# GpSimd takes q's product with its decay, the state's decay and small copies in a gated linear attention kernel

## The chip, the cores and the metric

The kernel runs on one core of one Trainium2 chip. The metric is the device time of one execution in microseconds (us); the median of three runs of the kernel before is 304.74 us (304.49 to 304.91). A core has five engines that work from queues of their own and wait for each other by semaphores: TensorE (in the profile PE, its weight loads PEld), VectorE (DVE), ScalarE (ACT), GpSimd (POOL) and SyncE (SP), which here issues the DMAs.

## The reference

Four sequences of 768 tokens with 8 heads of 48 features go through a gated linear attention and then through a block with a convolution and a gate:

```
f = 1 / (1 + exp(-f_logit))
for t in range(768):                                  # per sequence and head
    state = f[t][:, None] * state + outer(k[t], v[t]) # 48 x 48
    y[t] = q[t] @ state
x = y with the heads side by side                     # 768 x 384
h = max(x @ w_in, 0)                                  # 768 x 1024
conv = sum over 3 taps of conv_w[tap] * h shifted along the tokens
out = (h * sigmoid(conv)) @ w_out                     # 768 x 384
```

## The kernel before, in words

The attention is worked in 24 chunks (n = 0 to 23; four sequences of six chunks with 128 tokens each, c = 0 to 5 within a sequence). Per chunk, ScalarE turns the logits into ln(1 + exp(-f)) (L530, L534), and these are summed along the tokens, either by TensorE with a triangular matrix (L556, the first nine chunks) or by a scan on VectorE (L563). ScalarE takes two exponentials of the sum: with a plus sign for k (L565) and with a minus sign for q (L567), into the two halves of one buffer `e`, of which there are two. k and q lie side by side in one buffer `kq`, 128 partitions x 1024 numbers, and VectorE multiplies it by `e` in one instruction (L572). The last column of q's exponential is the decay over the whole chunk; a copy keeps it in `ft_all` (L569).

TensorE turns k (L587) and multiplies k by q for the scores (L594). VectorE copies the scores under a mask (L602), a copy brings the turned k from PSUM (L598), TensorE forms the products of k and v (L622) and of the scores and v (L614). VectorE adds the state's two halves (L635, L638), and the state is multiplied by its decay (L642 on VectorE, or L644, four activations on ScalarE), which the next chunk's L635 and TensorE's carry (L658) read. The result leaves PSUM as a rounded part (L671) and a rest (L673).

Two halves of a sequence make eight units u. In each, eight blocks f of 128 hidden features are computed as nine matmuls with split weights (L711), clipped by ScalarE into `hb` (L721), convolved by one ScalarE and two VectorE instructions (L727, L731), and gated in pairs (L735, L737). `hb` has two columns ahead of the tokens: for the first half of a sequence they are set to zero (L698), for the second half they are copied from the end of the first (L701), and the clipping waits for that. The output takes 24 tiles with 24 matmuls each (L767), from a rounded part (L754) and a rest (L758) of the gated features, and a copy (L773) ahead of the DMA. The weights come as 64-bit floats and are split during the first 60 us (L411 to L458).

`ORDER` is a list, written out, of all 1231 operations by number. Each engine's queue is that list with the other engines' work left out; a letter behind a number chooses the engine where an operation may run on several, and a number behind the dot chooses the buffer. An engine that waits for one operation holds up all that stands behind it.

Of the kernel before, what the change touches and what calls it, by code (L numbers as in the profile page):

```python
# [55 lines left out]
342.0 853 789.1 788.1 372.1 373 343.0 814 133.1 374 330 725.1 809 131 726 331v 790 375 132 835 346 332 347 810 348  # L56
405.1 392v 827 352.0 360.0 828 333 387.2 801.0 349 370.2 815 829 334 350 361.0 800.0 791.1 376.0 816 792 378.0 585 407
793.1 358.1 583 802 586 377.0 854 134 406.1 830 582 795.1 587 849 359.1 794.1 584 408.1 882 409 393 135 796 840 379.1
362 425 396.0 363 803.1 380 364 817 365 366 797.0 883.0 381 423.0 367.1 397.0 410 426.0 382 368 870.1 411 884 836 427
394.1 841 869 855 384 395v.0 871 414.0 856 441.3 385 398 872.1 415.1 875.0 383 386 885 873 459 888.1 876 908 842 399  # L60
# [3 lines left out]
905 593 916 419v 900 442.1 461 912 906 451.1 446 421.0 435 137 436 860 463 478.0 917 953.1 138 861v.1 496 948.0 422  # L64
907 448.0 949 894 438 449.0 922.0 954 466.0 475.0 479 452 493.1 494 467.0 961.1 458.0 960 918 950.0 913 439 550 966.0
962 462 497.1 440 498 974.1 951 967 973 437v 919 952 979.0 920 975 453 929.1 481 464.1 454 980 514 465.0 484.0 480 455
512.3 468 549.1 500 955 476.3 987.0 923 976 862 456 515.0 485.1 596 992.1 986 930.1 598 988 989 977 981 925.0 956 516
978 968 982 469 470 532 482.0 472 924 957 483.0 503.0 993 612.2 486 941.0 595 504.0 926 599 518 471 473.1 969 931.1
927.1 487 499v 474 613 928 488 597 533.1 990 994 513.0 958 501.1 489 490 502v.0 614 521.0 983 530.0 505 942.0 594
943.0 959 1011 491 534 492 535 984 522.1 932 506 963 995 517 507 944 985 536 519.0 945.1 509 520.0 996 551.0 539.0 615  # L70
531.2 1037 523 935.1 946 991 616.1 1012.0 508 933.0 524 510 964 934 1043.1 525 1013 511 965 602 970 527 1044 971 537.1
548.3 997 1017.1 600 538v.0 604 998 601 937.0 605 972 1018 617 620.2 936.0 603 540.0 1014.1 938 1019 552 1020 554
1030.1 939.0 1024 1050 940 1045 1015 528.2 1025.0 1031 529 526 1021 1032 1016 541 618 1033 557.0 1022 542 555.0 558.1
# [921 lines left out]
```

## Time and profile before

| | |
|---|---|
| median of three runs | 304.74 us |
| span of the profiled execution, first to last instruction | 301.5 us |
| median less that span | 3.24 us |
| TensorE busy | 293.8 us, 97% |
| VectorE busy | 255.3 us, 85% |
| ScalarE busy | 241.5 us, 80% |
| GpSimd busy | 2.8 us, 1% |
| granted clock of TensorE, mean | 0.996 |

The profile gives the execution's own time as its span; what lies around it is known only as the difference to the runs. A busy engine is one with an instruction running. TensorE's matmuls overlap and their ends are modelled, so a busy TensorE isn't proof that it works at its peak. Idle time of TensorE has the instruction behind the arrow as its releaser.

### The profile page before, as it was taken

How to read it: one execution, taken by the hardware profiler on the slowest of the kernel's cores; microseconds unless marked ns; L12 is line 12 of the kernel's file. 1: busy time of each engine (PE TensorE's matmuls, PEld its weight loads, DVE VectorE, ACT ScalarE, POOL GpSimd, SP SyncE). 2: the span in 40 equal slices, each digit the busy share in tenths (PEclk: the TensorE clock that was granted, in tenths of full speed). 3: DMA queues.
4: the chain of work that ended last, by engine and by line, in shares of the span. 5: the costliest groups of instructions: out<-in, count | busy, mean ns of one | idle time of the engine just before them, and what ended most of it. 6: DMA issues, size and time to landing. Idle time of an engine off the chain costs nothing. (4 is left out here: it accounts for less than half of the span.)

```text
span 301.5 us, 10047 instructions
## 1 busy us (share of the span) xinstructions
PE 293.8 (97%) x4319; PEld 276.6 (92%) x4319; DVE 255.3 (85%) x413; ACT 241.5 (80%) x482; POOL 2.8 (1%) x16
## 2 busy tenths in 40 slices
PE   8989999999999999999999999999999999999994
PEld 5867798999999999999999999989999999999993
DVE  3788999999999998999999996778985498498740
ACT  5787989999957999989979965876957797779460
POOL 3000000000000000000000000000000000000000
PEclk9999999999999999999999999999999999999998
DMA  6995799501650337522462454356041620212511
GB/s 216 393 358 185 267 299 383 156 2 32 165 217 0 99 133 231 180 80 72 133 202 49 160 164 122 99 156 195 8 145 21 185 70 28 96 54 97 192 54 58
DMA packets 19268, 43.38 MB, mean 144 GB/s; under 512 B 2684, under 2 KB 10004, under 8 KB 19220
## 3 DMA queue, kind: packets, MB, share of 16 engines
q1 hardware_dynamic: 19076, 42.50, 42.9%
q8 instruction: 35, 0.57, 0.8%
q10 hardware_dynamic: 144, 0.20, 0.2%
q14 instruction: 13, 0.11, 0.1%
HBM read 35.61 MB, written 4.72 MB: 134 GB/s over the span
## 5 line engine op out<-in xcount | busy, mean ns | idle before, releaser
L711 PE MATMUL mm<-xT,wi 128*128 128x384 f32 x576 | 107.3, 340 | 0.1
L711 PEld LDWEIGHTS mm<-xT,wi 128*128 128x128 f32 x576 | 100.5, 188 | 1.1 <-ACT hb L721 0.2
L731 DVE SCALAR_TENSOR_TENSOR g<-hb,cw,g 128x384 f32<-128x384 f32 (+1 forms) x128 | 73.8, 613 | 8.2 <-ACT g L727 7.9
L767 PE MATMUL mm<-wo,gh 128*128 128x384 f32 x384 | 70.9, 337 | 0.0
L767 PEld LDWEIGHTS mm<-wo,gh 128*128 128x128 f32 x384 | 66.5, 188 | 0.3
L721 ACT ACTIVATE hb<-mm 128x384 f32<-128x384 f32 x64 | 31.2, 488 | 16.6 <-PE mm L711 16.1
L727 ACT ACTIVATE g<-hb,cw 128x384 f32<-128x384 f32 (+1 forms) x64 | 37.4, 613 | 2.1 <-DVE gl L758 1.9
L767 PE MATMUL mm<-wo,gl 128*128 128x384 f32 x192 | 37.2, 338 | 0.0
L758 DVE TENSOR_TENSOR gl<-g,gh 128x1024 fp32r<-128x1024 f32 (+2 forms) x28 | 29.5, 1065 | 8.1 <-ACT gh L754 6.0
L767 PEld LDWEIGHTS mm<-wo,gl 128*128 128x128 f32 x192 | 33.4, 188 | 0.1
L572 DVE TENSOR_TENSOR kq<-kq,e 128x1024 f32<-128x1024 f32 x24 | 29.1, 1214 | 5.1 <-DMA kq<-in_kq_dram 5.1
L737 DVE SCALAR_TENSOR_TENSOR g<-g,hb 128x768 f32<-128x768 f32 (+1 forms) x32 | 30.1, 955 | 2.8 <-ACT g L735 2.5
L754 ACT CAST gh<-g 128x1024 fp32r<-128x1024 f32 (+2 forms) x28 | 25.8, 932 | 7.8 <-PE mm L767 4.6
L735 ACT ACTIVATE g<-g 128x768 f32<-128x768 f32 (+1 forms) x32 | 26.4, 840 | 0.0
L614 PE MATMUL Y<-am,v 64*64 64x64 f32 (+1 forms) x768 | 23.6, 219 | 0.0
L602 DVE COPY_PREDICATED am<-mask,S 128x512 f32<-128x512 uint8 x24 | 17.6, 733 | 1.9 <-PE S L594 1.8
L614 PEld LDWEIGHTS Y<-am,v 64*64 64x64 f32 (+1 forms) x768 | 18.8, 127 | 0.0
L673 DVE TENSOR_TENSOR xT<-Y,xT 112x512 fp32r<-112x512 f32 x24 | 16.3, 681 | 2.1 <-ACT xT L671 2.1
L563 DVE TENSOR_TENSOR_SCAN fb<-runs,fb 128x512 f32<-128x512 f32 x15 | 18.0, 1213 | 0.0
L594 PE MATMUL S<-kq 48*64 48x64 f32 x768 | 16.7, 221 | 1.0 <-DVE kq L572 0.9
L622 PEld LDWEIGHTS Y<-v,kp 64*48 64x48 f32 (+1 forms) x704 | 13.6, 127 | 3.5 <-issue 2.5
L594 PEld LDWEIGHTS S<-kq 48*64 48x64 f32 x768 | 13.9, 134 | 3.1 <-DVE kq L572 2.0
(100 smaller groups left out, 351.0 us busy)
## 6 DMA issues: line engine op xcount, KB each, us to landing
kq<-in_kq_dram SPq DMA_DIRECT2D x23, 512.0 KB, 6.0
v<-in_v_dram SPq DMA_DIRECT2D x24, 192.0 KB, 5.5
out_dram<-ob SPq DMA_DIRECT2D x23, 192.0 KB, 2.4
kq<-in_moe_w_in_dram SPq DMA_DIRECT2D x6, 512.0 KB, 5.1
kq<-in_moe_w_out_dram SPq DMA_DIRECT2D x6, 512.0 KB, 4.2
...
```

What stands on the lines that cost most here:

```text
L572: ox = plan.op("DVE", 1222, lambda e, X=X, E=E: nc.vector.tensor_tensor(buf(X), buf(X), buf(E), ALU.mult), ka, need=[o2] + ld_x, use=[X, E])
L594: o = nc.tensor.matmul(scores()[t, j, p, :], buf(X)[r, 0, p, t], buf(X)[r, 1, p, t], start=True, stop=True)
L614: o = nc.tensor.matmul(out_of(Y, p, j, w, z), buf(V).rearrange("p h d -> p (h d)")[t, h * D:h * D + w], buf(AM)[t, j, p, :], start=x == 1 ...
L711: nc.tensor.matmul(buf(ph)[:, :HS], wi[:, t, wl, f * P:(f + 1) * P], x_view(pl, u)[:, t, xl, :], start=(i == 0), stop=(i == 3 * KT - 1))
L721: nc.scalar.activation(hb[:, 2:HS + 2], buf(ph)[:, :HS], AF.Relu, scale=0.5)
L727: o = pl.op("ACT", 620, lambda e, cv=cv, hb=hb, n=n, f=f: nc.scalar.activation(cv(), hb[:, 1:n + 1], AF.Copy, scale=cw[:, 1, f:f + 1]), ke ...
L731: o = pl.op("DVE", 617, lambda e, cv=cv, hb=hb, n=n, f=f, w=w, sh=sh: nc.vector.scalar_tensor_tensor(cv(), hb[:, sh:n + sh], cw[:, w, f:f ...
L735: o = pl.op("ACT", 846, lambda e, cv=cv: nc.scalar.activation(cv(), cv(), AF.Tanh), key, need=last, use=[("g", u)], mode="T")
L737: gates[u, fp] = pl.op("DVE", 960, lambda e, cv=cv, fp=fp, n=n: nc.vector.scalar_tensor_tensor(cv(), cv(), 1.0, h_b[:, fp:fp + 2, 1:n + 1] ...
L754: o = pl.op("ACT", 180 + 110 * nn * NF // 128, lambda e, hv=hv, src=src: nc.scalar.copy(hv(), src()), key, need=[gates[v, fp] for fp in ra ...
L758: los.append(pl.op("DVE", 150 + 134 * nn * NF // 128, lambda e, hv=hv, lv=lv, src=src: nc.vector.tensor_tensor(lv(), src(), hv().bitcast(F ...
L767: nc.tensor.matmul(buf(po)[:, :DM], view(g)[:, f, :], wo[:, f, wl, :], start=(i == 0), stop=(i == 3 * NF - 1))
```

## The change

- L572 becomes two instructions, q's half and k's half. q's half runs on GpSimd in all 24 chunks, k's on VectorE. k's half needs k's exponential alone. The scores (L594) need both, the carry (L658) q's, the turn of k (L587) k's.
- The copy into `ft_all` (L569), the state's decay (L642, L644) and the two columns of `hb` (L698, L701) run on GpSimd, each in one instruction, in all chunks and units: 24 copies, 20 decays, 16 memsets and 16 copies.
- The rests of the gated features (L758) may run on GpSimd by the new code, but the new order leaves all of them on VectorE.
- The new `ORDER` has 1255 operations. The remaining work stands in the same order on TensorE, VectorE, ScalarE and SyncE as before, the exponentials of L565 and L567 among it.

```diff
+    copy_on = dict(ACT=nc.scalar.copy, DVE=nc.vector.tensor_copy, POOL=nc.gpsimd.tensor_copy)
+    tt_on = dict(DVE=nc.vector.tensor_tensor, POOL=nc.gpsimd.tensor_tensor)
+    memset_on = dict(DVE=nc.vector.memset, POOL=nc.gpsimd.memset)
...
-        keep = plan.op(dict(ACT=190, DVE=110), 0, lambda e, E=E, b=b, c=c: (nc.scalar.copy if e == "ACT" else nc.vector.tensor_copy)(
+        keep = plan.op(dict(ACT=190, DVE=110, POOL=200), 0, lambda e, E=E, b=b, c=c: copy_on[e](
             ft_all[:, b, c, :], buf(E)[:, 1, :, P - 1]), ka, need=[o2], use=[E])
-        ox = plan.op("DVE", 1222, lambda e, X=X, E=E: nc.vector.tensor_tensor(buf(X), buf(X), buf(E), ALU.mult), ka,
-                     need=[o2] + ld_x, use=[X, E])
+        oq, ox = [plan.op(dict(DVE=690, POOL=1300), 0, lambda e, X=X, E=E, z=z: tt_on[e](
+            buf(X)[:, z], buf(X)[:, z], buf(E)[:, z], ALU.mult), ka, need=[o2 if z else o1] + ld_x, use=[X, E], new=z == 1) for z in (1, 0)]
...
-        o = plan.op("PE", 490, score, (n, "sc"), need=[ox], use=[X], take=[("S", SC)], mode="q", n=64)
+        o = plan.op("PE", 490, score, (n, "sc"), need=[oq, ox], use=[X], take=[("S", SC)], mode="q", n=64)
...
-                if e == "DVE":
-                    return nc.vector.tensor_tensor(new, new, ft, ALU.mult)
+                if e != "ACT":
+                    return tt_on[e](new, new, ft, ALU.mult)
...
-            stated[n] = plan.op(dict(ACT=760, DVE=353), 0, decay, ks, need=[o, keep])
+            stated[n] = plan.op(dict(ACT=760, DVE=353, POOL=600), 0, decay, ks, need=[o, keep])
...
-                    oe = pl.op("DVE", 100, lambda e, fp=fp: nc.vector.memset(h_b[:, fp:fp + 2, 0:2], 0.0), key,
+                    oe = pl.op(dict(DVE=100, POOL=100), 0, lambda e, fp=fp: memset_on[e](h_b[:, fp:fp + 2, 0:2], 0.0), key,
...
-                    oe = pl.op(dict(ACT=200, DVE=110), 0, lambda e, fp=fp: (nc.scalar.copy if e == "ACT" else nc.vector.tensor_copy)(
+                    oe = pl.op(dict(ACT=200, DVE=110, POOL=200), 0, lambda e, fp=fp: copy_on[e](
                         h_b[:, fp:fp + 2, 0:2], h_b[:, fp:fp + 2, HS:HS + 2]), key, need=[gates.get((u - 1, fp))])
```

## Rows read from the trace of the kernel before

**Rows 1.** The page's head and its busy time (us, share, instructions).

```profile
span 301.5 us, 10047 instructions
...
PE 293.8 (97%) x4319; PEld 276.6 (92%) x4319; DVE 255.3 (85%) x413; ACT 241.5 (80%) x482; POOL 2.8 (1%) x16
```

**Rows 2.** Windows: stretch, us, busy us of PE, PEld, DVE, ACT, POOL; clock, DMA.

```profile
25.00:110.00 85.00, 84.68 (x1399) 77.20 (x1398) 84.52 (x133) 75.59 (x163) 0.00 (x0) 1.00 0.51 169
110.00:180.00 70.00, 69.91 (x1287) 67.21 (x1286) 67.46 (x106) 64.50 (x117) 0.00 (x0) 1.00 0.44 140
180.00:301.50 121.50, 116.90 (x1236) 114.38 (x1234) 87.03 (x140) 83.43 (x161) 0.00 (x0) 0.99 0.31 98
```

**Rows 3.** Groups by line and form, whole span: count, busy us, mean ns, idle before.

```profile
L572 DVE TENSOR_TENSOR kq<-kq,e 128x1024 f32<-128x1024 f32 x24 | 29.1, 1214 | 5.1 <-DMA kq<-in_kq_dram 5.1
...
L644 ACT ACTIVATE st<-st,ft_all 112x48 f32<-112x48 f32 x64 | 16.2, 329 | 0.7 <-DVE st L638 0.7
...
L569 ACT COPY ft_all<-e 128x4 f32<-128x4 f32 x22 | 4.1, 198 | 0.0
```

**Rows 4.** Groups by line on VectorE, 25 to 110 us.

```profile
L572 DVE TENSOR_TENSOR kq<-kq,e 128x1024 f32<-128x1024 f32 x10 | 12.1, 1216 | 0.0
...
L602 DVE COPY_PREDICATED am<-mask,S 128x512 f32<-128x512 uint8 x9 | 6.6, 733 | 0.0
L673 DVE TENSOR_TENSOR xT<-Y,xT 112x512 fp32r<-112x512 f32 x9 | 6.1, 682 | 0.3 <-ACT xT L671 0.3
...
L635 DVE TENSOR_TENSOR sh<-Y,st 112x192 f32<-112x192 f32 x7 | 2.4, 344 | 0.0
...
L638 DVE TENSOR_TENSOR st<-Y,sh 112x192 f32<-112x192 f32 x6 | 2.1, 346 | 0.0
...
L698 DVE MEMSET hb<- 128x4 f32 x7 | 0.4, 62 | 0.0
```

**Rows 5.** Groups by line on VectorE, 110 to 180 us.

```profile
L572 DVE TENSOR_TENSOR kq<-kq,e 128x1024 f32<-128x1024 f32 x8 | 9.7, 1212 | 0.7 <-DMA kq<-in_kq_dram 0.7
...
L642 DVE TENSOR_TENSOR st<-st,ft_all 112x192 f32<-112x192 f32 x3 | 1.1, 350 | 0.0
```

**Rows 6.** Groups by line and form on GpSimd, whole span.

```profile
L357 POOL MEMSET fg<- 128x512 f32 x2 | 1.0, 524 | 0.0
...
L785 POOL MEMSET mid<- 128x1 f32 x1 | 0.1, 98 | 0.0
```

**Rows 7.** Timeline, setup: start us, us, engine, line, operation, [idle before, releaser].

```profile
2.24 1.22 DVE L316 CAST idr<-ident 128x128 fp32r<-128x128 f32 x1
...
2.31 0.99 POOL L357 MEMSET fg<- 128x512 f32 x2
...
10.90 0.20 DVE L412 TENSOR_SCALAR gh<-gh 24x128 f32<-24x128 f32 x1
```

**Rows 8.** Timeline where TensorE waits, or nearly waits, for the products.

```profile
8.23 1.22 DVE L572 TENSOR_TENSOR kq<-kq,e 128x1024 f32<-128x1024 f32 x1 [4.40 <-DMA kq<-in_kq_dram]
...
12.21 0.59 ACT L567 ACTIVATE e<-mm 128x512 f32<-128x512 f32 x1
...
19.66 0.69 PE L594 MATMUL S<-kq 48*64 48x64 f32 x32 [0.53 <-DVE kq L572]
...
30.67 2.35 DVE L572 TENSOR_TENSOR kq<-kq,e 128x1024 f32<-128x1024 f32 x2
...
31.69 1.12 PE L452 MATMUL mm<-gh,ident 128*128 128x512 f32 x2 [0.26 <-ACT wi L457]
...
33.11 0.63 PE L587 MATMUL Y<-ident,kq 128*128 128x128 f32 x4
...
102.18 1.22 DVE L572 TENSOR_TENSOR kq<-kq,e 128x1024 f32<-128x1024 f32 x1
...
104.69 0.51 PE L594 MATMUL S<-kq 48*64 48x64 f32 x21
...
197.37 0.69 PE L594 MATMUL S<-kq 48*64 48x64 f32 x32 [0.33 <-DVE kq L572]
```

More of the change, by code (lines that the diff above doesn't have):

```diff
@@ L35 @@
 ORDER = """
[20 rows of a table removed]
[L56 to L60, printed above, removed]
[3 rows of a table removed]
@@ L64 @@
[L64 to L73, printed above, removed]
@@ L74 @@
-1026 1056.1 1027 1023 1028 1038.0 1089 543 1057 1029 556.0 544v 1058 1046 559 1063.0 619 545 624.1 560 1039 1034 561
[9 rows of a table removed]
-622 1204 1164 1145.1 1165 646 1146 1150 1213.0 1219.1 1214.1 1215.1 1151v.1 623 643 647 1152 1216 1205.0 1207 1221.0
-1217.0 1206.1 656.2 648.1 1218 1220.0 1208 1222 1225.1 1209.1 1223.1 1226.0 1224 655 649 1210 657 1227.0 658 650 659
-651 660 661.0 662 1211.1 1212 1228 1229v.0 1230
+91.0 92 93 139.0 158.1 45.0 94 100.1 96 140.0 7.1 159.1 97.1 23.1 95.0 10.0 24 141.0 4.0 142.0 8.1 177.2 143 5.0 98
@@ new lines @@
+160.1 145p 146v 99.0 102 6.0 144p 149.0 46.0 161.1 147.0 150.0 162 179.0 47 148.0 48 164p 165v 3.0 180.0 151 181 49
+50.0 168.0 103 51 687p 152 9.0 34.0 153 101 169.1 166.1 35 155 52 167.0 178.2 53.0 154p 109.0 25.0 0.0 196.0 104.0 54
+26 11.0 156.0 170 111 157 107 234.3 198.1 163p 182p 171 28 183p 184v 172 187.0 199.0 27.0 55.2 185.0 188.0 105 106.0
+29.0 1.0 186.0 217.0 173p 36.1 189 108.1 200 174 218.1 190 112 236.1 191 215.1 201p 219 37 197.1 175 56 193 113.0 110
+176 30.0 251.2 202p 203v 216.0 12.3 38.0 237.0 206.0 238 40.1 204.1 194 32.1 31 195 39 207.0 592 253.0 726p 240p 241v
@@ new lines @@
+116 13 33 593 192p 41.1 221p 222v 588 205.0 239p 591 220p 713p 58.0 254.0 223.0 57.0 255 225.0 59 117.1 589 208 42 65
+226.1 291.0 61 209 60 256p 114 2.0 292.1 43.1 62 224.0 210 590 115.0 63 293 64 212 257p 258v 244.0 235.2 213.1 123.1
+227 14.1 44 124 272.0 211p 214 125 118.0 245.0 73.0 242.1 273.0 228 15 714.1 120 274 243.0 83 67.0 17 16.0 82 719.0
+229 715 119 68 230p 246 18.0 720 70 231 247 261.0 66.1 232 270.1 248 71 289.0 126 233 21.0 262.1 249 700p 69 127 19.1
+250 72 594 22 259.0 252.0 20 84.0 727.0 271.2 85.0 308.3 121 87 598 688.1 597 86 728 595 122 276p 277v 693.0 599 689
@@ new lines @@
+596 310 275p 690.0 290.3 706.1 260.0 691 694 295p 296v 695 701.0 716 692 721 717 707 278.1 311.0 696 263 294p 718 702
+312 697 280.0 264 722 732.0 698 281.0 265 314p 315v 299.0 279.0 267 699 266p 282 268.0 300.1 757.1 751p 729 269 733
+723 703 283 724 297.0 730 752.0 284 298.0 704 734 725 708 301 758 705 285p 318.0 709 777p 286 731 753 88 302 778.0 735
+287 303 710 313p 754.1 736 711 305 288 737 783.1 712 402.3 779 738 306 780 307 796.0 759 755 764p 603 790p 784 760 601
+756 791.1 602 797 761 785 605 781 798 604 316.0 786 792 600 770.0 782 762 347.2 787 346.2 793 799 74 788 765.1 363.0
@@ new lines @@
+763 327.1 771 328.0 794 304p 309.1 800 830.0 772 795 766 829p 789 801 835.1 831 802 767 773 869.0 836 768 868p 76.1
+769 856.1 870 77 855p 774 79 874.0 75.1 857 80 775 78 861.1 875 776 81 843.0 862 319.0 803.1 89 848.1 805 842p 90 844
+329 807.0 804v.0 330.0 331 806v 745.0 333p 334v 808 317.0 365 739.1 320 348 809.0 332p 366.1 810 337.0 849 335.1
+740v.1 741.1 336.0 321 349.0 746v.0 367 350 338.1 832.0 128.0 322 742 837 129 352p 353v 850 876 403 324 845 368p 871
+356.0 384 382.3 339 325.0 130 811.1 747.0 369p 370v 323p 846 351p 404.0 847 863 326 858 748 340 405 872 743.0 357.0
@@ new lines @@
+823.0 744 354.0 877 813.1 812v.1 385.1 386 355.0 838 133.1 387p 341 749.1 833 131 750 342p 814 388p 389v 132 859 358
+343 359 834 360 420.1 406p 851 364.0 373.0 852 344 401.2 825.0 361 383.2 839 853 345 362 374.0 824v.0 815.1 390.0 840
+816 392.0 609 422 817.1 371.1 607 826 610 391.0 878 134 421.1 854 606 819.1 611 873 372.1 818v.1 608 423.1 906p 424
+407p 408v 135 820 864 393.1 375 441 411.0 376 827.1 394 377 841 378p 379 821.0 907.0 395 439.0 380.1 412.0 425p 442.0
+396 381 894.1 426p 427v 908 860 443 409.1 865 893p 879 398 410v.0 895 430.0 880 458.3 399 413 896.1 431.1 899.0 397p
@@ new lines @@
+400 909 897 477 912.1 900 932p 866 414 901 428.0 867 444p 933.0 913 460 887.0 925.1 445p 446v 934 429.0 415 461.0 898
+449.0 919p 496 926 432 914 417 416p 902 920.1 478.1 910 440.3 462 828 888v.1 935 136.0 418 433 938.0 464p 465v 475.2
+921 927 881.1 903 889.1 915 922 419 904 911 614 939 434 616 905 615 890 450.0 515.2 882v.0 447.1 891.1 436 448.0 892
+916 945.0 612 468.0 928 822 451 923 917 613 883.0 971p 929 617 940 435p 924 459.1 479 936 930 469.1 463p 437.0 452 137
+453 884 481p 482v 497.0 941 977.1 138 885v.1 516 972.0 438 931 466.0 973 918 455 467.0 946v.0 978 485.0 494.0 498 470
@@ new lines @@
+513.1 514 486.0 985.1 476.0 984p 942 974.0 937 456 573 990.0 986 480p 517.1 457 518 998.1 975 991 997p 454p 943 976
+1003.0 944 999 471 953.1 500p 501v 483.1 472 1004 535 484.0 504.0 499p 473 533.3 487 572.1 520p 521v 979 495.3 1011.0
+947 1000 886 474 536.0 505.1 620 1016.1 1010p 954v.1 622 1012 1013 1001 1005 949.0 980 537 1002 992 1006 488 489 554
+502.0 491 948v 981 503.0 524.0 1017 636.2 506 965.0 619 525.0 950 623 539p 540v 490p 492.1 993 955.1 951.1 507 519p
+493 637 952 508 621 555.1 1014 1018 534.0 982 522.1 509p 510 523v.0 638 543.0 1007 552.0 526 966v.0 618 967.0 983
@@ new lines @@
+1035p 511 556 512 557p 1008 544.1 956 527 987 1019 538p 528 968 1009 558p 559v 541.0 969.1 530 542.0 1020 574.0 562.0
+639 553.2 1061p 545 959.1 970 1015 640.1 1036.0 529p 957.0 546 531 988 958 1067.1 547 1037 532 989 626 994 549 1068
+995 560.1 571.3 1021 1041.1 624 561v.0 628 1022 625 961.0 629 996 1042 641 644.2 960v.0 627 563.0 1038.1 962 1043 575
+1044 577p 578v 1054.1 963.0 1048p 1074p 964 1069 1039 550.2 1049.0 1055 551 548p 1045 1056 1040 564 642 1057 581.0
+1046 565 579.0 582.1 1050 1080.1 1051 1047 1052 1062.0 1113p 566 1081 1053 580.0 567p 1082 1070 583 1087.0 643 568
@@ new lines @@
+648.1 584 1063 1058 585 1064 1071 1119.0 1065 656.3 1083 1066 1088v.0 1114.1 1120 1059 1072 1060 1075.0 1115 1073
+1132.1 1084 1076 586 1077 1145.0 1078 1126p 1079 1133 569 1139p 587 1127.1 1146 1085 1086 1140.0 1128 649 570 1089 634
+1153.1 1141 630 650 652.0 1023.1 651 1091.0 1152p 1090v 660.1 657 635 1154 631 633 632 1092 1029.0 1158.1 1093.0
+1030v.0 653 1094 1024v.1 1031.0 1159 661 1116.0 1142 1117 1147 1143 1155 1025.1 1148 1121 1144 1129 1149 662 1118 658
+1122 1150 1032 1156 1123 1107.0 1151 1026 1033.0 663 1124 1034 1157 664.1 1209.0 1027.1 1125 654 1134 1130 1178.1
@@ new lines @@
+1203p 1131 1210 1177p 1160 1101.1 1161 1204.0 1162 1179 1135 1109.1 1108v.0 1205 1163 1164 1136 1217.0 659 1095.0
+1216p 1137 1096v.1 1110 1218 1138 1097.0 1111.0 1102v.0 1112 676.3 1180.1 1190p 1219 1191.1 665 1165.0 1098 1192 1206
+1207 1222.1 1099.0 1220 1193 1100 1181 1211 1028 655 1196.0 1223 1208 1212 1103.1 1194 1197 1182 1224 1221 576p 1198
+1225 677 1166v.1 645 1104 1171.1 1213 1199 678 1183.0 1105.1 1200 1106 1195 668.0 1172v.0 1167.1 1184 666 1226 1185
+1201 1186 1214 1202 1168 1227 1215 669 1173.0 1187 646 1228 1188 1169.1 1189 670 1170 1174 1237.0 1243.1 1238v.1
@@ L87 @@
+1239.1 1175v.1 647 667 671 1176 1240 1229.0 1231 1245.0 1241.0 1230v.1 680.2 672.1 1242 1244v.0 1232v 1246 1249.1
+1233.1 1247.1 1250v.0 1248 679 673 1234 681 1251.0 682 674 683 675 684 685.0 686 1235.1 1236 1252 1253v.0 1254
 """
@@ L109, in ring, with op @@
         self.rings[name] = [(ap, frozenset(cells)) for ap, cells in bufs]
-    def op(self, eng, ns, run, key, need=(), take=(), use=(), mode=None, size=0, n=0, behind=()):
+    def op(self, eng, ns, run, key, need=(), take=(), use=(), mode=None, size=0, n=0, behind=(), new=False):
         engs = eng if isinstance(eng, dict) else {eng: ns}
         o = Op(engs=engs, run=run, at=key, key=(self.when(key), len(self.ops)), need=[x for x in need if x is not None],
-               take=list(take), use=list(use) + [i for _, i in take], mode=mode, size=size, n=n, after=None, behind=list(behind))
+               take=list(take), use=list(use) + [i for _, i in take], mode=mode, size=size, n=n, after=None, behind=list(behind), new=new)
         o.need += [x for x in o.behind if x not in o.need]
@@ L138, in fixed @@
             i, _, k = w.partition(".")
-            o = self.ops[int(i.rstrip("v"))]
-            o.on = "DVE" if i[-1] == "v" else next(iter(o.engs))
+            o = self.ops[int(i.rstrip("avp"))]
+            o.on = {"a": "ACT", "v": "DVE", "p": "POOL"}.get(i[-1]) or next(iter(o.engs))
+            assert o.on in o.engs, w
             for r, t in o.take:
@@ L662, in carry @@
             return first, first
-        ov = carried[n] = plan.op("PE", 710 if c else 490, carry, kv, need=[stated[n - 1] if c else None, oh, ox],
+        ov = carried[n] = plan.op("PE", 710 if c else 490, carry, kv, need=[stated[n - 1] if c else None, oh, oq],
                      behind=[new_s] if new_s else [], use=[X, V, AM, Y], mode="q",
@@ L757, in moe @@
                     his.append(o)
-                    los.append(pl.op("DVE", 150 + 134 * nn * NF // 128, lambda e, hv=hv, lv=lv, src=src: nc.vector.tensor_tensor(
+                    los.append(pl.op(dict(DVE=150 + 134 * nn * NF // 128, POOL=250 + 280 * nn * NF // 128), 0, lambda e, hv=hv, lv=lv, src=src: tt_on[e](
                         lv(), src(), hv().bitcast(F32), ALU.subtract), key, need=[o], use=[gh, ("g", v)] + ([gl] if t0 else []),
```

32 rows, old and new, of the table ORDER are left out of this document.

## The prediction

> **What bounds the kernel now.** I read the page's busy line first, then the busy time in three stretches, then the groups by line, and last the timeline at the places where TensorE idles. TensorE is busy for 293.8 of 301.5 us [rows 1], so it is the bound, and all its idle time together is 7.7 us. In the stretches [rows 2] the reader is to see two different regimes. From 25 to 110 us TensorE is busy 84.68 of 85.00 us, and VectorE 84.52: VectorE idles for 0.48 us in 85, and works through a fixed list in which every delay is handed on to the next entry. From 110 to 180 us it idles for 2.54 us, and from 180 us on for 34.5. ScalarE is busy 75.6 of 85 us in the first stretch. GpSimd does nothing after its 2.8 us of setup. So a change here is worth at most what TensorE idles, a few us, and what it may cost depends on VectorE in the first two stretches.
>
> Span and time: the profiled execution spans 301.5 us, the median of the runs is 304.74, so 3.24 us lie around the span. No step of the change touches the start or the end of the program, so I add the change of the span to the median.
>
> **The change part by part.** *Off ScalarE:* the state's decay, four activations in each of 16 chunks, 16.2 us; the copies for the last column of the exponential, 22 of them, 4.1 us [rows 3]; and 16 copies of two columns of hb. TensorE never waits long for ScalarE: the one place that I count is an idle 0.26 us at 31.69 us, where a matmul of the weight split waits for a copy [rows 8]. The rest of the relief is worth nothing while VectorE is the later of the two.
>
> *Off VectorE:* the product of k and q with the exponentials is one instruction of 1024 elements, 1214 ns, in each of 24 chunks [rows 3]. It becomes one of 512 for k. The nearest rows for that size are 682 ns (L673) and 733 ns (L602) [rows 4]; I take 690, so VectorE saves 0.53 us a chunk. Sixteen memsets of 62 ns go too, seven of them in the first stretch [rows 4], and in the second stretch three decays of 350 ns [rows 5].
>
> *Onto GpSimd:* 24 products for q, 20 decays, 24 + 16 small copies, 16 memsets. No row shows a GpSimd product. Its nearest row is a memset of the same 128x512, 524 ns [rows 6], which moves one stream; a product moves three. Lower end 0.52 us (all streams at once), upper end 3 x 0.524 = 1.57 us (one after another); I take 1.1 us, two streams of reads in a row. The decay has 192 elements instead of 512: between 0.35 us, VectorE's price [rows 5], and 192/512 of 1.57, 0.59 us; I take 0.45. A small copy I put at 0.1 us, from the memset of one column, 98 ns [rows 6]. The Trainium skill, page "GPSIMD Engine Reference", section "Elementwise — side-by-side cycle accounting", gives 4497 ns for a two-input product of 2048 elements; a quarter of that is an estimate of 1.12 us, and no run here shows it yet.
>
> Is GpSimd in time by itself? New waits are: TensorE's score matmuls (L594) for q's product, with the transposes and the value matmuls queued behind them; TensorE's carry (L658) and VectorE's L635 for the decay; ScalarE's relu (L721) for the edge columns; and ScalarE's next exponential (L565) for the two readers of its buffer. In chunk 2, for instance, q's exponential ends at 12.80 us and the scores start at 19.66 [rows 8], so 1.1 us on an idle engine is hidden. In chunk 11 the product started as soon as the exponential was there, at 102.18, and the scores came at 104.69 [rows 8]: 2.5 us for 1.1. Only chunk 0 has no room: its product starts at 8.23 when the data land, lasts 1.22 us [rows 8], and the scores follow it. Two halves side by side would cost 0 there; one after the other, 0.69 + 1.1, cost 0.56.
>
> *The port.* The decisive price is not GpSimd's own time but what it does to VectorE. In the setup a cast of 128x128 took 1.22 us on VectorE while GpSimd ran memsets from 2.31 to 3.30 us; a tensor_scalar of as many elements per partition took 0.20 us when GpSimd was idle [rows 7]. The cast ended only after GpSimd's memsets had. So the two engines do hold each other up, at 1.0 us in that instance. That VectorE operation had one input in SBUF. Whether two-input operations are held as well, no row shows; if they are, GpSimd's reads stop VectorE wherever it would run one. The Trainium skill, page "SBUF — State Buffer", section "Who interferes with whom", says that they are: a VectorE instruction with two SBUF inputs is blocked by a GpSimd instruction that reads SBUF until that one has finished, and the other way round; by that rule the sum below holds, and without it the first rival does.
>
> How much of VectorE's work is exposed? Free of it is what reads only one operand from SBUF: L602, L673, L635, L638 and the memsets, 6.6 + 6.1 + 2.4 + 2.1 + 0.4 = 17.6 of 84.5 us [rows 2, 4]. So 79% of VectorE's time can be held, and I take 0.79 of GpSimd's reading time as lost to VectorE.
>
> From 25 to 110 us there are 10 products [rows 4], 7 decays (chunks 2 to 4 and 6 to 9) and 13 copies: 11.0 + 3.15 + 1.3 = 15.5 us of GpSimd, x 0.79 = 12.2 us of holding. VectorE saves 10 x 0.53 + 0.4 = 5.7. It falls behind by 6.5 us, has 0.5 of idle time to catch up, and TensorE has 1.3 us in hand late in this stretch (the product of chunk 11 ended at 103.40, its scores started at 104.69 [rows 8]): 4.7 us reach TensorE. Earlier there is less in hand still: the product that ended at 33.02 was used at 33.11 [rows 8].
>
> From 110 to 180 us: 8 products [rows 5], 6 decays, 12 copies: 8.8 + 2.7 + 1.2 = 12.7 us, x 0.75 (a little less, since scans and products are fewer per us) = 9.5. Saved: 8 x 0.53 + 1.1 + 0.4 = 5.7. Net 3.8, less 2.5 of idle time: 1.3 us. After 180 us VectorE's idle 34.5 us swallow the rest.
>
> At the ends: +0.56 in chunk 0; in chunk 2 the scores waited 0.53 us for the product, which is now shorter, -0.53; the same in chunk 22, idle 0.33 [rows 8], -0.33. Sum 4.7 + 1.3 - 0.3 = +5.7 us: a span of 307.2 and a time of 310.4 us.
>
> The order of the two exponentials, of which the title speaks, is not in the diff: k's (L565) stays ahead of q's (L567) in the written order of every chunk. I count nothing for it.
>
> **The rivals.** *First, no holding (the other side).* Two-input work of VectorE runs freely beside GpSimd. Then VectorE gains 0.53 us a chunk and TensorE loses only its waits for it: 0.53 at 19.66, 0.33 at 197.37 and 0.26 at 31.69 [rows 8], together 1.1: 303.6 us. For it: the only hold in the trace is of another kind of operation. Against it: 84.68 of 85 us of TensorE are work [rows 2], so nothing more than this can come. It decides from the point at which less than about a half of GpSimd's reading time is lost to VectorE: 15.5 x 0.5 = 7.7, less 5.7 saved, is 2.0, about the 1.8 us of idle time and margin.
>
> *Second, a draw.* The holding is there but about half of it falls on operations that don't mind; savings and losses cancel: 304.7, give or take 0.6.
>
> *Third, GpSimd is the one that waits.* If VectorE keeps the port and each product of q first waits out an instruction of up to 1.2 us, it takes some 2.4 us. VectorE loses nothing, chunk 0 starts its scores 1.1 us later, chunk 11 just makes it (102.18 + 2.4 against 104.69), and of the gains 0.2 remain: 305.6 us. For it: VectorE's list has no gaps in which GpSimd could get in. Against it: in the setup it was VectorE's cast that waited, and GpSimd's memsets kept their 0.5 us each [rows 7].
>
> **How the numbers follow.** Forecast 0.58, no holding 0.22, a draw 0.12, GpSimd late 0.08. The forecast's own range: with a product of 0.52 and a decay of 0.35 us the holding (9.0 x 0.79 = 7.1) is covered by savings and margins, and the time is about that of the draw; with 1.57, 0.59 and three times 0.1 us for a copy it is 11.3 + 6.7 = 18 us, 322. I give it 306 to 318. The whole range goes down to 303.4, which takes in most of the first rival, and up to 318. A measurement of this kernel can tell about 0.2%, 0.6 us, from no change. Slower is the forecast and the late GpSimd, 0.66; the same is the draw, 0.12; faster is the first rival, 0.22.
>
> **What would show it.** Right: in the profile after, L731, L737, L758 and L563 on VectorE have longer means than before, or instances of twice their length, wherever a GpSimd product runs; TensorE idles between 40 and 110 us behind VectorE or behind ScalarE's relu; L602 and L673 keep their 733 and 682 ns. Wrong: those means are unchanged and TensorE is still busy over 84 of the 85 us. GpSimd's rows for the product above 2 us with VectorE's unchanged would be the third rival. If GpSimd's product is near 0.6 us, my price was too high and the draw is due.

## The result and the profile after

The changed kernel takes 307.90 us (median of ten runs, 306.16 to 310.16) against 304.83 us of the kernel before (ten runs, 303.36 to 306.54): a ratio of 1.0103, with a 95% interval of 1.0071 to 1.0136. It is slower by about 3.1 us. I had forecast slower by 5.7. The sign was right and the size about twice too large. Of the mechanism one half came out, VectorE held by GpSimd's reads; about as much of the loss comes from GpSimd being late, which I had counted for chunk 0 alone.

The profiled execution of the changed kernel took 307.62 us with a span of 305.9, so 1.7 us lie around it. The 3.24 us that I had added to the span before hold some 1.5 us by which that one execution was shorter than its median. So the spans differ by 4.4 us and the medians by 3.1, and everything below that is read by comparing the two profiles adds up to the 4.4.

The line numbers of the changed kernel stand seven higher. First its head, its busy time and the three stretches (columns as in [rows 2]), to be laid beside [rows 1, 2]:

```profile
span 305.9 us, 10116 instructions
...
PE 294.3 (96%) x4319; PEld 276.8 (91%) x4319; DVE 256.6 (84%) x391; ACT 225.4 (74%) x380; POOL 93.7 (31%) x116
```

```profile
25.00:110.00 85.00, 81.55 (x1401) 73.69 (x1395) 80.36 (x120) 66.04 (x117) 36.13 (x35) 1.00 0.49 159
110.00:180.00 70.00, 69.26 (x1309) 66.64 (x1302) 68.65 (x98) 61.20 (x94) 31.37 (x32) 1.00 0.43 136
180.00:305.90 125.90, 121.58 (x1263) 119.18 (x1262) 92.19 (x142) 82.42 (x142) 16.28 (x24) 0.99 0.33 103
```

TensorE's work is the same. It idles 3.45 us of the first stretch instead of 0.32, 0.74 of the second instead of 0.09, and 4.32 of the third instead of 4.60. VectorE, which was to be relieved, is as busy as before over the span, 256.6 us against 255.3, and yet it now has 4.6 us of idle time in the first stretch, where it had 0.5. GpSimd is busy for 93.7 us, far more than the 41 us that the prices of the prediction give for its new work (24 x 1.1 + 20 x 0.45 + 40 x 0.1 + 16 x 0.1). Where that comes from stands in its groups by line:

```profile
L579 POOL TENSOR_TENSOR kq<-kq,e 128x512 f32<-128x512 f32 x24 | 39.2, 1633 | 52.5 <-ACT e L574 37.1 <-DMA kq<-in_kq_dram 15.3
L649 POOL TENSOR_TENSOR st<-st,ft_all 112x192 f32<-112x192 f32 x20 | 25.2, 1260 | 25.2 <-DVE st L645 25.2
L708 POOL COPY hb<-hb 128x4 f32<-128x4 f32 x16 | 15.2, 956 | 48.6 <-DVE g L744 48.6
L576 POOL COPY ft_all<-e 128x4 f32<-128x4 f32 x24 | 12.1, 512 | 5.6 <-ACT e L574 5.0 <-PE S L601 0.5
L705 POOL MEMSET hb<- 128x4 f32 x16 | 1.6, 102 | 37.0 <-DVE g L744 37.0
```

A copy of 4 elements per partition has a mean of 956 ns in one line and 512 in the other; the shortest instances of both take 0.18 us. The shortest products take 1.25 to 1.34 us (12 of 24), the shortest decay 0.50. What each instance takes beyond that adds up to about 44 us: 8.2 in the products, 15.2 in the decays, 8.0 and 12.4 in the copies. The memsets, which read nothing, have no such excess: 102 ns.

The same on VectorE, by line and form:

```profile
L738 DVE SCALAR_TENSOR_TENSOR g<-hb,cw,g 128x384 f32<-128x384 f32 x64 | 41.0, 671 | 1.8 <-ACT g L734 1.6
L738 DVE SCALAR_TENSOR_TENSOR g<-hb,cw,g 128x385 f32<-128x385 f32 x64 | 37.9, 636 | 7.3 <-ACT g L734 7.1
L570 DVE TENSOR_TENSOR_SCAN fb<-runs,fb 128x512 f32<-128x512 f32 x15 | 22.1, 1480 | 0.3 <-ACT fb L541 0.3
L579 DVE TENSOR_TENSOR kq<-kq,e 128x512 f32<-128x512 f32 x24 | 19.8, 827 | 5.1 <-DMA kq<-in_kq_dram 5.1
L609 DVE COPY_PREDICATED am<-mask,S 128x512 f32<-128x512 uint8 x24 | 17.6, 734 | 4.3 <-PE S L601 4.3
L680 DVE TENSOR_TENSOR xT<-Y,xT 112x512 fp32r<-112x512 f32 x24 | 16.2, 679 | 0.0
```

In the kernel before, the convolution steps and the scan were:

```profile
L731 DVE SCALAR_TENSOR_TENSOR g<-hb,cw,g 128x384 f32<-128x384 f32 x64 | 37.2, 610 | 1.9 <-ACT g L727 1.8
L731 DVE SCALAR_TENSOR_TENSOR g<-hb,cw,g 128x385 f32<-128x385 f32 x64 | 36.6, 615 | 6.3 <-ACT g L727 6.1
...
L563 DVE TENSOR_TENSOR_SCAN fb<-runs,fb 128x512 f32<-128x512 f32 x15 | 18.0, 1213 | 0.0
```

The operations with two inputs in SBUF (L738, L570, L579) have longer means: 671 and 636 ns for 610 and 615, 1480 for 1213, and 827 for k's half, whose shortest instances take 0.67 us. The two that read one of their inputs from PSUM keep 734 and 679 ns [rows 4]. The excess adds up to about 16 us in some 23 instances, of 0.2 to 1.5 us each. Beside all of them runs a GpSimd instruction that reads, and in all but 1.2 us of the excess one of the products. So 16 us of waiting lie on VectorE and 44 on GpSimd, and of the 44 only 8.2 on the products. (These sums were made from the instances of the trace: each one's duration less that of the short instances of its line and form. A profile's spans on GpSimd are rough; that the long ones are real is seen from what starts right behind them.)

Both directions can be read in the timeline (start, duration, engine, line, operation, idle time before). First GpSimd held, at chunk 4:

```profile
31.16 1.28 DVE L579 TENSOR_TENSOR kq<-kq,e 128x512 f32<-128x512 f32 x2
32.36 0.56 DVE L423 TENSOR_SCALAR gh<-g 128x768 int32<-128x768 int32 x1
32.83 0.56 DVE L421 TENSOR_SCALAR gl<-g 128x768 int32<-128x768 int32 x1
33.30 0.95 DVE L426 SCALAR_TENSOR_TENSOR gh<-g,gh 128x768 int32<-128x768 int32 x1
...
31.11 3.50 POOL L649 TENSOR_TENSOR st<-st,ft_all 112x192 f32<-112x192 f32 x1
34.58 1.25 POOL L579 TENSOR_TENSOR kq<-kq,e 128x512 f32<-128x512 f32 x1
...
35.89 0.69 PE L601 MATMUL S<-kq 48*64 48x64 f32 x32 [1.64 <-POOL kq L579]
```

The decay of chunk 2 starts beside VectorE's two products and ends at 34.61, just after the last of five VectorE instructions that follow one another without a gap (33.30 + 0.95 = 34.25): 3.50 us for work of 0.50. Behind it in GpSimd's queue stands the product for the scores, and TensorE idles 1.64 us. And the copies of hb's columns, in the block of unit 1:

```profile
76.92 4.11 POOL L708 COPY hb<-hb 128x4 f32<-128x4 f32 x2 [4.13 <-DVE g L744]
78.25 2.73 DVE L738 SCALAR_TENSOR_TENSOR g<-hb,cw,g 128x385 f32<-128x385 f32 x5
81.06 0.49 ACT L728 ACTIVATE hb<-mm 128x384 f32<-128x384 f32 x1 [2.33 <-POOL hb L708]
81.60 1.14 PE L718 MATMUL mm<-xT,wi 128*128 128x384 f32 x5 [0.30 <-ACT hb L728]
```

Two copies, 0.36 us of work, end after 4.11 us, at 81.03, when the last of five convolution steps has ended (78.25 + 2.73 = 80.98); the clipping on ScalarE starts at 81.06, after 2.33 us of waiting, and TensorE waits 0.30. Then VectorE held, three times:

```profile
15.21 0.51 POOL L649 TENSOR_TENSOR st<-st,ft_all 112x192 f32<-112x192 f32 x1 [2.59 <-DVE st L645]
15.60 1.74 DVE L441 TENSOR_TENSOR c<-gh,gl 24x128 f32<-24x128 f32 x1
15.66 0.31 POOL L576 COPY ft_all<-e 128x4 f32<-128x4 f32 x2
15.93 1.27 POOL L579 TENSOR_TENSOR kq<-kq,e 128x512 f32<-128x512 f32 x1
17.40 0.24 PE L491 MATMUL mm<-ident,c 24*128 24x24 f32 x1 [1.02 <-DVE c L441]
...
62.07 1.34 POOL L579 TENSOR_TENSOR kq<-kq,e 128x512 f32<-128x512 f32 x1 [1.34 <-ACT e L574]
62.19 2.69 DVE L738 SCALAR_TENSOR_TENSOR g<-hb,cw,g 128x384 f32<-128x384 f32 x3
64.81 0.71 DVE L609 COPY_PREDICATED am<-mask,S 128x512 f32<-128x512 uint8 x1
65.62 0.69 PE L601 MATMUL S<-kq 48*64 48x64 f32 x32 [1.16 <-issue]
...
118.39 1.32 POOL L649 TENSOR_TENSOR st<-st,ft_all 112x192 f32<-112x192 f32 x1 [0.92 <-DVE st L645]
119.28 2.09 DVE L738 SCALAR_TENSOR_TENSOR g<-hb,cw,g 128x384 f32<-128x384 f32 x1
119.68 1.27 POOL L579 TENSOR_TENSOR kq<-kq,e 128x512 f32<-128x512 f32 x1
121.69 0.46 PE L665 MATMUL Y<-kq,sh 48*48 48x64 f32 x16 [0.74 <-DVE sh L642]
```

An addition of 24x128 elements, 0.27 us in the kernel before (at 14.34), shows 1.74 us: from 15.21 to 17.20 GpSimd runs a decay, two copies and a product, one behind the other, and the addition ends 0.14 us after the last of them. The transpose that needs it comes 1.02 us late. At 62.19 three convolution steps take 2.69 us, where three in the kernel before take 1.67 (at 58.78), with a product beside the first. The masked copy behind them ends at 65.52, and the scores of chunk 8, for which it frees the one buffer `S`, start 0.10 us later. The profile names no releaser for their 1.16 us. At 119.28 a convolution step of some 0.61 us takes 2.09, with the product's 1.27 us in it; the state that TensorE's carry needs is next on VectorE, and the carry waits 0.74 us. A hold has no row of its own: it is read from an instruction that is too long for its shape.

### The profile page after: what moved, and what is told of

The parts are those of the page before. It is cut to its first block, busy times and chain, and to the rows that moved or that the text cites. A ratio compares the mean times of both kernels' runs of the same rounds, so it can differ in the third digit from the quotient of the medians.

```text
span 305.9 us, 10116 instructions
## 1 busy us (share of the span) xinstructions
PE 294.3 (96%) x4319; PEld 276.8 (91%) x4319; DVE 256.6 (84%) x391; ACT 225.4 (74%) x380; POOL 93.7 (31%) x116
## 4 chain that ended last, share of the span: by engine, by line
PE 66%; DVE 17%; POOL 4%; ACT 4%; issue 4%; DMA 3%; SPq 0%; POOLq 0%; ACTq 0%
PE mm L774 28%; PE mm L718 23%; DVE g L738 5%; PE Y L665 3%; PE S L601 3%; PE Y L621 3%; PE Y L629 2%; PE Y L594 2%; DMA kq<-in_kq_dram 2%; DVE fb L570 2%; POOL kq L579 2%; DVE am L609 2%; DVE g L744 1%; DVE kq L579 1%; POOL hb L708 1%
## 5 line engine op out<-in xcount | busy, mean ns | idle before, releaser
L738 DVE SCALAR_TENSOR_TENSOR g<-hb,cw,g 128x384 f32<-128x384 f32 (+1 forms) x128 | 79.0, 654 | 9.1 <-ACT g L734 8.7
L579 POOL TENSOR_TENSOR kq<-kq,e 128x512 f32<-128x512 f32 x24 | 39.2, 1633 | 52.5 <-ACT e L574 37.1
L765 DVE TENSOR_TENSOR gl<-g,gh 128x1024 fp32r<-128x1024 f32 (+2 forms) x28 | 29.8, 1075 | 8.1 <-ACT gh L761 6.0
L649 POOL TENSOR_TENSOR st<-st,ft_all 112x192 f32<-112x192 f32 x20 | 25.2, 1260 | 25.2 <-DVE st L645 25.2
L744 DVE SCALAR_TENSOR_TENSOR g<-g,hb 128x768 f32<-128x768 f32 (+1 forms) x32 | 30.9, 979 | 2.1 <-ACT g L742 1.9
L708 POOL COPY hb<-hb 128x4 f32<-128x4 f32 x16 | 15.2, 956 | 48.6 <-DVE g L744 48.6
L579 DVE TENSOR_TENSOR kq<-kq,e 128x512 f32<-128x512 f32 x24 | 19.8, 827 | 5.1 <-DMA kq<-in_kq_dram 5.1
L570 DVE TENSOR_TENSOR_SCAN fb<-runs,fb 128x512 f32<-128x512 f32 x15 | 22.1, 1480 | 0.3 <-ACT fb L541 0.3
L609 DVE COPY_PREDICATED am<-mask,S 128x512 f32<-128x512 uint8 x24 | 17.6, 734 | 4.3 <-PE S L601 4.3
```

The lines of the kernel that those rows point to most:

```text
L570: o = plan.op("DVE", 1240, lambda e, fv=fv: nc.vector.tensor_tensor_scan(fv(), runs, fv(), 0.0, ALU.mult, ALU.add), ka, need=[gate[n]], us ...
L579: oq, ox = [plan.op(dict(DVE=690, POOL=1300), 0, lambda e, X=X, E=E, z=z: tt_on[e](buf(X)[:, z], buf(X)[:, z], buf(E)[:, z], ALU.mult), ka ...
L738: o = pl.op("DVE", 617, lambda e, cv=cv, hb=hb, n=n, f=f, w=w, sh=sh: nc.vector.scalar_tensor_tensor(cv(), hb[:, sh:n + sh], cw[:, w, f:f ...
L744: gates[u, fp] = pl.op("DVE", 960, lambda e, cv=cv, fp=fp, n=n: nc.vector.scalar_tensor_tensor(cv(), cv(), 1.0, h_b[:, fp:fp + 2, 1:n + 1] ...
L765: los.append(pl.op(dict(DVE=150 + 134 * nn * NF // 128, POOL=250 + 280 * nn * NF // 128), 0, lambda e, hv=hv, lv=lv, src=src: tt_on[e](lv( ...
```

## The experiments

The theory was that GpSimd's reads and VectorE's operations with two SBUF inputs exclude each other, both ways, and that this alone makes the loss. One rival was that nothing is held (the first of the prediction) and that GpSimd's own price and the new waits make it; another that the split into two instructions or the new place of the work is at fault.

**The disputed price by itself.** On top of the kernel before, GpSimd gets spare work from chunk 9 on, for which nobody waits and whose result nobody uses: two products in each of 15 chunks in the one kernel, two memsets in place of each product in the other.

```diff
+            if (b, c) >= steps[9]:
+                pace, spare = [t for t, _ in plan.rings["fg"]]
+                nc.gpsimd.tensor_copy(pace[:, :NP], ft_all[:, b, c, :])
+                for _ in range(2):
+                    nc.gpsimd.tensor_tensor(spare, runs, runs, ALU.mult)   # d_read
+                    # d_write: nc.gpsimd.memset(spare, 1.0), twice
```

> The kernel before, with two products of 128x512 on GpSimd beside each of the chunks 9 to 23 (30 in all, from about 60 us on); both inputs are one constant tile in SBUF, the result goes to a buffer that nobody reads any more, and a copy of four columns ahead of them ties them to their chunk. Nothing waits for them. Port held both ways: about half of 30 x 1.3 = 39 us of GpSimd's reading holds VectorE, some 15 to 20 us, none of it paid back by a shorter product; VectorE has about 3 us of idle time before 180 us, so TensorE loses 4 to 10 us: 309 to 315 us, with L731, L737, L758 and L563 longer by up to 1.3 us in single instances and L602, L673 unchanged. Rival, no port, only GpSimd's own lateness and its queue: 304.8 us within 0.6, all of VectorE's durations unchanged.

> The same as the run with the spare products, but each product is two memsets of 128x512 on GpSimd (60 in all, 524 ns each), which read nothing; the copy of four columns that ties them to their chunk stays. Port held by reads alone: VectorE's two-input operations are not held, 304.8 us within 0.6, means of L731, L563 within 2% of before. Rival, any GpSimd work holds VectorE: as slow as the run with the products, 309 us or more. No port at all: 304.8 as well.

Measured: 313.61 us for the reads, ratio 1.0350 (1.0316 to 1.0384), and 303.50 us for the memsets, ratio 0.9992 (0.9973 to 1.0011). Of the reading kernel, groups by line on VectorE and GpSimd:

```profile
L739 DVE SCALAR_TENSOR_TENSOR g<-hb,cw,g 128x384 f32<-128x384 f32 (+1 forms) x128 | 82.8, 682 | 7.9 <-ACT g L735 7.5
L580 DVE TENSOR_TENSOR kq<-kq,e 128x1024 f32<-128x1024 f32 x24 | 31.3, 1307 | 5.0 <-ACT fb L530 4.9
L610 DVE COPY_PREDICATED am<-mask,S 128x512 f32<-128x512 uint8 x24 | 17.6, 732 | 1.0 <-PE S L602 0.8
L575 POOL TENSOR_TENSOR fg<-runs 128x512 f32<-128x512 f32 x30 | 43.4, 1446 | 1.2
```

Of the writing kernel:

```profile
L740 DVE SCALAR_TENSOR_TENSOR g<-hb,cw,g 128x384 f32<-128x384 f32 x64 | 37.2, 612 | 1.9 <-ACT g L736 1.8
...
L581 DVE TENSOR_TENSOR kq<-kq,e 128x1024 f32<-128x1024 f32 x24 | 29.1, 1214 | 4.0 <-ACT e L567 4.0
L563 DVE TENSOR_TENSOR_SCAN fb<-runs,fb 128x512 f32<-128x512 f32 x15 | 18.1, 1216 | 0.6 <-issue 0.6
```

The first rival falls: work that no one waits for costs 3.5% when it reads, in us within the expected range and as a ratio just above it (315 is 1.033 of 304.83). With the reads VectorE's two-input means go from 612 to 682 and from 1214 to 1307 ns, and its masked copy from PSUM stays at 732; the scan, which I had expected to be held too, keeps 1214. With memsets none of these moves. The excess on VectorE is 15.9 us in 26 instances, 51% of the 30 x 1.04 us that the products would take unheld (their shortest instances take 1.04 us; both their inputs are one tile). On GpSimd the products wait 12.3 us and the pacing copies 6.2. The Trainium skill, page "SBUF — State Buffer", section "Who interferes with whom", says that a VectorE instruction with two SBUF inputs contends with a GpSimd instruction that reads SBUF and not with one that only writes; the two ratios agree with it.

**The parts one by one**, each on GpSimd alone with the rest as before.

```diff
 p_prod:  ORDER of the changed kernel without the "p" on decay, last column and columns of hb
 p_edge:  ORDER of the kernel before, "p" on the last column and on both forms of hb's columns
 p_decay: ORDER of the kernel before, "p" on the state's decay
```

> The changed kernel with the decay, the copies of the last column and the edge columns back on ScalarE and VectorE as before; only q's product is on GpSimd. Port theory: VectorE is held by the 24 products for about 13 us and saves 13, so it is no later than before; the score matmuls of chunk 4 no longer wait behind a decay (1.7 us of the loss go), the clipping no longer behind a copy (1.0 us go): 304 to 306 us, nearer to 305. Rival, the price is GpSimd's instruction time (1.3 us against 1.21 on VectorE) on the way to the scores: the same waits as in the changed kernel, 307 us or more. If the products alone are the cost, 307.5 to 309.

> The kernel before with only the small ones moved to GpSimd: 24 copies of the last column, 16 memsets and 16 copies of the edge columns; product and decay as before. Port theory: each copy of four columns takes 0.18 us alone but waits behind VectorE's trains of two-input operations, up to 3 us; ScalarE's clipping waits for the edge copies, TensorE for the clipping, at two places of unit 1 and 2 by together 1 us: 305 to 306.5 us. Rival, no port: the copies cost 0.18 us each and have 1.5 us or more in hand: 304.2 to 304.9 us.

> The kernel before with the state's decay alone on GpSimd, in all 20 chunks; the product in one instruction and the small copies as before. ScalarE is relieved of 16 us, VectorE of 1.4. Port theory: a decay takes 0.50 us alone and up to 3.5 us behind a train of VectorE; it has 2 us and more in hand in most chunks; VectorE is held only where the decay gets in first, some 4 us in all, about 2 of them in the saturated stretches: a ratio of 1.001 to 1.005. Rival, no cost and ScalarE's relief counts: 0.996 to 0.999.

Measured: the product 306.47 us, ratio 1.0081 (1.0051 to 1.0112); the copies and memsets 304.38 us, 1.0036 (1.0018 to 1.0053); the decay 304.11 us, 1.0021 (1.0001 to 1.0041). The product is the main part; the sum, 1.38%, is over the 1.03% of the whole, but within what the intervals allow. As ratios, the copies and the decay lie in the ranges of the theory. The product doesn't: on the 304.83 us of the result 1.0081 is 307.3, the place of that run's rival and not the 304 to 306 of the theory. What I had foreseen for it did go, the stall of chunk 4 and those behind the copies; but VectorE is held for 15.4 us, not 13, each time beside a product, and TensorE loses time at other places, chunk 8 (0.96 us) and chunk 0 (some 0.6) among them. With the copies alone VectorE keeps its 612 ns, and TensorE's loss is in the blocks of units 1 and 2 (0.33 and 0.49 us), where ScalarE's clipping waits for a held copy. With the decay alone:

```profile
L646 POOL TENSOR_TENSOR st<-st,ft_all 112x192 f32<-112x192 f32 x20 | 31.8, 1590 | 182.5 <-DVE st L642 178.7 <-ACT hb L725 3.8
```

Here the mean is three times the 0.50 us of a free decay, and the kernel loses 0.2%. GpSimd's waiting is dear only where something is queued behind it. The three kernels also show who waits. The 40 copies alone wait 20 us and hold VectorE nowhere; the 20 decays alone wait 22 us and hold it for 1.9; the 24 products alone wait 8.9 us and hold it for 15.4. The short instructions, 0.18 and 0.50 us, nearly only wait; the long ones, 1.29 us, hold VectorE more than they wait.

**The product without its reads.** The kernel with the product alone, but it leaves q's product out: GpSimd copies four columns and then sets q's half by two memsets. The split, the waits and the place stay.

```diff
-            buf(X)[:, z], buf(X)[:, z], buf(E)[:, z], ALU.mult)            # q's half
+            nc.gpsimd.tensor_copy(buf(X)[:, 1, :, P - 1], buf(E)[:, 1, :, P - 1])
+            nc.gpsimd.memset(buf(X)[:, 1], 0.05)
+            return nc.gpsimd.memset(buf(X)[:, 1], 0.05)
```

> The run with the product alone on GpSimd, but q's product is left out: GpSimd copies four columns of q's exponential (so that it waits for it as before) and then sets q to a constant by two memsets of 128x512, 1.05 us, which read nothing. VectorE's half product, the waits of the scores for GpSimd and the queue are as they were; the q that is used isn't the reference's. Port theory (GpSimd's reads and VectorE's two-input operations hold each other): nothing of 0.5 us or more is held on VectorE, VectorE keeps the 13 us that it saves, and TensorE loses only some of its waits for the product: 303 to 304.3 us where the kernel before has 304.5, a ratio of 0.994 to 0.999. Rival (GpSimd as a stage of its own ahead of the scores is what costs, or the split in two): a ratio of 1.005 to 1.009 as with the product.

Measured: 303.68 us, ratio 1.0012 (0.9992 to 1.0031), against 1.0081 with the reads; I had expected 0.994 to 0.999. Two rows of its groups, and two of its timeline:

```profile
L744 DVE SCALAR_TENSOR_TENSOR g<-hb,cw,g 128x384 f32<-128x384 f32 x64 | 37.3, 611 | 2.1 <-ACT g L740 1.8
...
L583 POOL MEMSET kq<- 128x512 f32 x24 | 12.6, 526 | 1.4
...
33.34 0.85 POOL L584 MEMSET kq<- 128x512 f32 x1
33.64 0.96 DVE L421 TENSOR_SCALAR gl<-g 128x768 int32<-128x768 int32 x1
```

So the reads make nearly all of the product's loss; the split and GpSimd's stage ahead of the scores, which lasts about as long as the product, are not at fault. It shows a second thing: VectorE saves its 0.54 us in each of 24 chunks here, 13 us, all but unspoilt, and the time doesn't fall. In its trace TensorE gains at the places that the prediction names, 0.16 us in chunk 2, 0.42 at the weight split and 0.54 in chunk 22, and the scores of chunk 0, behind GpSimd's stage, lose 0.7. Of 13 us about 1.1 reach TensorE, and the new stage takes most of that back. The last two rows are one of two places, 0.8 us in all, where a VectorE operation with one input is held beside a memset, as the cast of [rows 7] was: 0.96 us for 0.55. Here the memset is held as well, 0.85 us for 0.52.

**The order on GpSimd.** The changed kernel, with GpSimd's product of chunk 5 moved behind the decay of chunk 2 and the product of chunk 4. My theory was that the 1.64 us of chunk 4 came from the order of GpSimd's queue and could be had back.

```diff
-... 253.0 726p 240p 241v
-116 13 33 593 192p 41.1 221p 222v ...
+... 253.0 726p 241v 116
+13 33 593 192p 41.1 221p 240p 222v ...
```

> The changed kernel with one entry moved in GpSimd's queue alone: the product of chunk 5 behind the decay of chunk 2 and the product of chunk 4, instead of ahead of them; every other queue is the same. Theory that the largest single loss (the scores of chunk 4, 1.7 us) comes from an entry that waits for its exponential at the head of GpSimd's queue while VectorE is about to run a train: decay and product are done before 29 us, the wait of the scores at 35.9 us is gone, 306 to 306.7 us, 1.2 to 1.7 us faster than the changed kernel (ratio about 1.005). Rival, VectorE's work and not the queue makes the scores of chunk 4 late: no more than 0.4 us faster (ratio about 1.009 to 1.010).

Measured: 307.09 us, ratio 1.0122 (1.0093 to 1.0150): no better than the 1.0103 of the changed kernel. The theory fell. The timeline of this kernel:

```profile
29.50 6.26 POOL L579 TENSOR_TENSOR kq<-kq,e 128x512 f32<-128x512 f32 x2 [1.82 <-DMA kq<-in_kq_dram]
...
34.53 0.69 PE L601 MATMUL S<-kq 48*64 48x64 f32 x32
...
36.98 1.16 PE L563 MATMUL mm<-tri,fg 128*128 128x128 f32 x8 [1.07 <-ACT fg L541]
```

The scores of chunk 4 come at 34.53 without a wait, but the same train of VectorE instructions now holds the product of chunk 5 (two products in 6.26 us, for 2.6 us of work). The copies of the last column stand behind it, ScalarE's next exponential waits 2.4 us for them, and TensorE loses 1.07 us two microseconds further on. Here the train holds whatever GpSimd has next.

**An attempt to beat both.** The kernel before, with GpSimd only where VectorE has time: hb's memsets, and q's product of chunk 22 alone.

```diff
+        oq, ox = [... for z in (slice(1, 2), slice(0, 1))] if n == 22 else [plan.op("DVE", 1222, ...)] * 2
```

> A version meant to beat the kernel before: on GpSimd only what reads nothing (the 16 memsets of the edge columns) and the product of q in chunk 22, where TensorE waited 0.33 to 0.54 us for VectorE and VectorE has idle time around it; all else as before. Port theory: the memsets cost nothing, the scores of chunk 22 start some 0.5 us earlier: a ratio of 0.997 to 0.999, at the edge of what can be told. Rival, any product on GpSimd costs more than it gives: 1.001 or more.

Measured: 303.89 us, ratio 1.0010 (0.9985 to 1.0035), where I had expected 0.997 to 0.999. No gain that can be told from none. Its trace shows where the 0.5 us went:

```profile
194.68 1.30 POOL L576 TENSOR_TENSOR kq<-kq,e 128x512 f32<-128x512 f32 x1 [22.96 <-DMA kq<-in_kq_dram]
195.06 1.33 DVE L738 SCALAR_TENSOR_TENSOR g<-hb,cw,g 128x384 f32<-128x384 f32 x1
```

The one product falls beside a convolution step, which takes 1.33 us for 0.61. That is more than the 0.54 that k's half saves VectorE behind it, and TensorE idles 0.59 us ahead of the scores of chunk 22, for 0.33 in the kernel before.

## Why the prediction was right, and where its size was off

**The savings** were sized right: k's half takes about 0.67 us where it isn't held, 0.54 less than the 1214 ns of the whole [rows 3]; I had 0.53.

**The prices on GpSimd** were too low: the product 1.29 us for 1.1, the decay 0.50 for 0.45, the copy 0.18 for 0.1. The estimate of 1.12 us from the Trainium skill, page "GPSIMD Engine Reference", section "Elementwise — side-by-side cycle accounting", was too low as well for this kernel's products; the page's own time is that of an addition. In the two stretches from 25 to 180 us the free prices make 18 x 1.29 + 13 x 0.50 + 25 x 0.18 = 34.2 us of reading, for 28.2 in the prediction. By itself that would have made the forecast worse.

**The failed step** is "I take 0.79 of GpSimd's reading time as lost to VectorE". Measured: about 11.4 us of holds on VectorE from 25 to 180 us, a third of those 34.2; I had 12.2 + 9.5 = 21.7. The step took the share of VectorE's time that can be held as the share of GpSimd's time that is lost to VectorE, for every instruction alike, and let all the waiting fall on VectorE. The runs show two shares. The decays and copies, 8.4 of the prediction's 28.2 us, hold VectorE next to never; where VectorE's instructions follow one another without a gap they wait instead, 36 of the 44 us over the span, and at the places shown to the end of the train. The products hold it for about half of their time and not for 0.79: 12.1 us from 25 to 180 us in the kernel with the product alone, 52% of 18 x 1.29, and 51% in the reading kernel. The setup row [rows 7], in which VectorE's cast waited and GpSimd's memsets didn't, had suggested that VectorE is the one that waits. Why the products get in between more often than the decays and copies is not shown; they differ in length and in kind.

**The balance.** 11.4 us held against 11.4 saved (5.7 in each stretch): by VectorE's balance alone it was the draw of the second rival. That the time still lies in the forecast's range is in part luck: the prices were too low, the share was too high by more, and a loss that I had not counted filled the gap. It is 3.1 us slower for two reasons. A saving of 0.54 us a chunk reaches TensorE at three places only, as the product without reads shows, while a hold of over a microsecond reaches it wherever less than that is in hand. And GpSimd is late itself, as the third rival said, though at other places than chunk 11. By place, in the two profiles, TensorE's difference is:

| where | us |
|---|---|
| GpSimd late: scores of chunk 0 and 4, blocks of units 1 and 2 behind the copy of hb's columns | 0.43 + 1.68 + 0.55 + 0.48 = 3.14 |
| VectorE held: transpose at 17.40, scores of chunk 8, carry of chunk 11 | 1.09 + 1.23 + 0.90 = 3.22 |
| gains: scores of chunk 2 and 22, weight split at 31.69 [rows 8] | -0.43 - 0.54 - 0.42 = -1.39 |
| other stalls of before that are gone: products of k and v at 17.43, scores and carry of chunk 14 | -0.85 - 0.35 = -1.20 |
| k and q of chunk 0 landing at 8.89 instead of 8.23 | 0.72 |

The sum is 4.5, beside 4.4 of span. The three gains stand at the places of the first rival (0.53, 0.33 and 0.26). That of chunk 22 isn't the shorter product's alone: the kernels with the copies or the decay alone, where the product is whole, have it too. The wait of chunk 8 comes with the reads: the kernel with the product alone and the one with the other order have it, with the scores again 0.11 us behind the masked copy, and the product without reads doesn't. The last two rows I don't put down to the change. The product of chunk 0 starts between 7.85 and 9.00 us in the ten profiles: at 8.79 in the reading kernel, which begins like the kernel before, and at 8.22 in the one with the other order, which begins like the changed one. The stall of chunk 14 is gone too in the kernel of the last experiment, which has nothing new near it. The one at 17.43, of 0.60 us in the middle of a group of matmuls and without a releaser, is there in seven of the ten profiles, with up to 1.09 us; its cause stays open.

**What was to show it** did: L738, L744 (in one form, 1004 ns for 955) and L570 have longer means, L609 and L680 keep theirs, and TensorE idles behind VectorE and behind ScalarE's clipping. The mean of L765 (L758 before) does not change, 1218 ns in both: most of it runs late, where GpSimd has little to do. There the forecast's list of what to see was wrong.
